# Resetting the tally that shares PSUM evictions between ACT and DVE at each item, and moving one block of weight transposes behind the last attention value

## The chip, the cores and the metric

One core of one Trainium2 chip. The metric is device time in microseconds, the median of several executions; the kernel before takes 173.48 us (173.47 to 173.84 in 3 runs). Profiles show one execution, whose span is some 2 us shorter than the device time. Every profiled run was in the fast state, at a granted TensorE clock of 0.995 to 1.000.

In this document PE is TensorE (PEld its weight loads), ACT is ScalarE, DVE is VectorE, POOL is GpSimd and SP is the engine that issues most stores and DMA transposes. "L581" is line 581 of the kernel. The PSUM tiles h_ps, k_ps, v_ps, s_ps and o_ps hold the maxout product, the k sort, the v sort, the scores and the values; g, kT, v_sb, e and x are what is made of them outside of PSUM.

## The reference, cut to what matters

```python
def attention(q, k, v, sort_net):            # (4, 8, 768, 64), 8 blocks of 96
    P = sort_net
    for _ in range(5):                       # Sinkhorn: rows, then columns
        ...
    k_sorted, v_sorted = P @ k_blocks, P @ v_blocks
    scores = scale * q_b @ k_sb.T            # inside each block
    return softmax(scores) @ v_sb

x = attention(...).transpose(0, 2, 1, 3).reshape(3072, 512)
g = maximum(x @ w1, x @ w2)                  # 512 -> 1024
out = g @ w_out                              # 1024 -> 512
```

## The kernel before

The kernel works on four items (b = 0 to 3). While PE computes the output layer of item b, it also does the attention of item b + 1 in small steps. The maximum is split as x w2 + relu(x (w1 - w2)), so that relu(x (w1 - w2)) is the g tile and the rest is one product with W2 W_out (`wc`), which the first item computes from transposed W2 (`w2T`).

Three things matter here. First, all products go through the same four PSUM tiles of 4 KB per partition:

```python
psum = ctx.enter_context(tc.tile_pool(name="psum", bufs=4, space=bass.MemoryType.PSUM))
def ps_f32(name):
    return psum.tile([128, 1024], FP32, tag="ps", name=name)
```

So a new product waits until an older tile has been copied out ("evicted") by ACT or DVE. Second, a tally decides at build time which of the two does it:

```python
load = {"A": 0.0, "D": 0.0}

def pick(a_ns, d_ns):
    if load["A"] + a_ns <= load["D"] + d_ns:
        load["A"] += a_ns
        return "A"
    load["D"] += d_ns
    return "D"

def evac(out_ap, in_ap, n, two_x=False, eng=None):
    a_ns, d_ns = (200 + n) / 1.2, (130 + (n / 2 if two_x else n)) / 0.96
    if eng:
        load[eng] += a_ns if eng == "A" else d_ns
    if (eng or pick(a_ns, d_ns)) == "A":
        nc.scalar.copy(out=out_ap, in_=in_ap)
    else:
        nc.vector.tensor_copy(out=out_ap, in_=in_ap)
```

Other work is charged as well: each exp of scores adds 800 to "A", each normalized value 900 to "D", each piece of turning v into the layout of the sort 800 to "D". Third, in the first item the second half of W2 is transposed on PE and copied out in two halves, on ACT and on DVE (`w2_transposes(1, "AD")`), among the last values of the first item:

```python
tail = {
    ...
    3: [
        VA[6],                                    # values: product, then 1/sum and x on DVE
        lambda: w2_transposes(1, "AD")(),
        VA[7],
        lambda: x_transposes(0, 2, "A"),
        ...
    ],
    4: [lambda: x_transposes(0, 3, "A"), load_rest, lambda: turn(second, 36)],
    ...
}
...
for b in range(B):
    units = [... moe_h(b, 0, t) ..., moe_h(b, 1, t) ..., moe_out(b, ti, part) ...]
    ...
    steps, lo = [], 2
    ...
```

The softmax here doesn't subtract the row's maximum and nothing guards it: scores larger than these inputs give would overflow.

## Time and profile before

| | before |
|---|---|
| device time, median | 173.48 us |
| span of the profiled run | 171.4 us |
| PE busy | 161.7 us (94%) |
| ACT busy, DVE busy | 83.7 and 87.9 us (49%, 51%) |
| PE idle from 72 to 91 us | 1.93 us |

The shares of ACT and DVE over the whole run look perfectly balanced.

What one eviction costs is read from the groups on the page of the kernel before. The columns are line, engine, operation, output and input tile, shapes, count, then busy us and mean ns of one, then the idle time ahead of them:

```profile
L595 ACT ACTIVATE g<-h_ps 128x768 bf16<-128x768 f32 x23 | 18.6, 812 | 17.4 <-PE h_ps L581 17.4
L597 DVE TENSOR_SCALAR g<-h_ps 128x768 bf16<-128x768 f32 x9 | 8.6, 956 | 25.5 <-PE h_ps L581 25.5
L105 DVE CAST v_sb<-v_ps 96x1024 bf16<-96x1024 f32 x7 | 8.3, 1214 | 4.1 <-PE v_ps L398 3.3
L103 ACT CAST v_sb<-v_ps 96x1024 bf16<-96x1024 f32 x9 | 8.8, 1020 | 1.6 <-PE v_ps L398 1.6
```

An eviction costs 0.14 to 0.19 us more on DVE than on ACT, for the same tile. The tally's formula gives 1.02 and 1.20 us for 1024 elements, so its costs are right; what it is ignorant of is when the charged work happens. The views of the stretches, of the chain and of the waits are shown in the prediction.

### The profile page before, as it was taken

What the parts mean: (1) busy time and instruction counts of PE and PEld (TensorE: products, weight loads), DVE (VectorE), ACT (ScalarE), POOL (GpSimd) and SP (SyncE); (2) the same over time, 40 slices, a digit from 0 to 9 for tenths busy, and PEclk for the clock granted to TensorE, in tenths of its full rate; (3) what the DMA queues carried; (4) which work ended last, traced back from release to release, by engine and by line L of the source; (5) the groups of instructions that cost most, each with busy time, mean ns of one, the idle gap of its engine ahead of it and who ended that gap; (6) DMA issues with size and microseconds to landing.
All of it is one profiled execution on the core that took longest, in us unless ns stands there. A gap on an engine that the chain in (4) does not pass through costs nothing.

```text
span 171.4 us, 4548 instructions
## 1 busy us (share of the span) xinstructions
PE 161.7 (94%) x2015; PEld 96.6 (56%) x2015; DVE 87.9 (51%) x194; ACT 83.7 (49%) x102; POOL 24.8 (14%) x40
## 2 busy tenths in 40 slices
PE   7699999999999999998889999999999999999992
PEld 7548676736666554456555455575545445654462
DVE  5879668499556399810485644225472232420040
ACT  4599975846645554069764253275605214231001
POOL 7955362242300000000320000000000000000000
PEclk9999999999999999999999999999999999999999
DMA  4999999999999452992099267950023273000333
GB/s 49 201 205 207 199 207 206 207 205 207 213 222 196 76 168 54 193 232 96 4 174 189 54 168 145 195 183 4 2 50 77 91 205 130 6 0 0 122 122 126
DMA packets 29811, 23.11 MB, mean 135 GB/s; under 512 B 16672, under 2 KB 24736, under 8 KB 29792
## 3 DMA queue, kind: packets, MB, share of 16 engines
q0 software_dynamic: 10304, 12.58, 43.1%
q1 hardware_dynamic: 19200, 10.04, 23.2%
q8 instruction: 16, 0.26, 0.6%
q10 hardware_dynamic: 288, 0.20, 0.4%
q14 instruction: 3, 0.02, 0.0%
HBM read 25.17 MB, written 6.29 MB: 184 GB/s over the span
## 4 chain that ended last, share of the span: by engine, by line
PE 80%; DVE 10%; ACT 6%; issue 2%; DMA 1%; DVEq 0%; ACTq 0%
PE out_ps L608 37%; PE h_ps L581 22%; PE o_ps L471 4%; PE wc_ps L559 3%; PE k_ps L377 3%; PE s_ps L444 3%; ACT v_sb L103 2%; PE v_ps L398 2%; DVE v_sb L105 1%; ACT kT L103 1%; DVE x L488 1%; PE tw_ps L529 1%; PE tq_ps L347 1%; PE tq_ps L352 1%; ACT g L595 1%
## 5 line engine op out<-in xcount | busy, mean ns | idle before, releaser
L608 PE MATMUL out_ps<-wo_sb,g 128*128 128x512 bf16 (+2 forms) x208 | 48.3, 363 | 0.0
L581 PE MATMUL h_ps<-xT,w_sb 128*128 128x384 bf16 x256 | 44.8, 326 | 2.1 <-DVE v_sb L105 0.7
L581 PEld LDWEIGHTS <-w_sb 128*128 128x128 bf16 x256 | 24.2, 98 | 17.5 <-issue 2.0
L452 ACT ACTIVATE e<-s_ps 96x768 bf16<-96x768 f32 x32 | 24.2, 808 | 16.7 <-PE s_ps L444 16.6
L595 ACT ACTIVATE g<-h_ps 128x768 bf16<-128x768 f32 x23 | 18.6, 812 | 17.4 <-PE h_ps L581 17.4
L608 PEld LDWEIGHTS <-g 128*128 128x128 bf16 x208 | 17.6, 97 | 15.2
L608 PE MATMUL out_ps<-wc,xT 128*128 128x512 bf16 (+2 forms) x104 | 25.0, 362 | 0.0
L103 ACT COPY o<-out_ps 128x1024 f32<-128x1024 f32 x10 | 10.1, 1012 | 29.3 <-PE out_ps L608 24.7
L488 DVE TENSOR_TENSOR x<-o_ps,rs 96x512 bf16<-96x512 f32 x32 | 22.0, 687 | 1.1
L597 DVE TENSOR_SCALAR g<-h_ps 128x768 bf16<-128x768 f32 x9 | 8.6, 956 | 25.5 <-PE h_ps L581 25.5
L482 DVE RECIPROCAL rs<-o_ps 96x8 f32<-96x8 f32 x32 | 6.4, 200 | 21.4 <-PE o_ps L471 21.4
L608 PEld LDWEIGHTS <-xT 128*128 128x128 bf16 x104 | 9.9, 97 | 11.0
L471 PEld LDWEIGHTS <-e 96*128 96x128 bf16 x256 | 11.6, 98 | 6.9 <-DVE x L488 0.7
L209 DVE COPY v_dc<-v_raw 64x768 bf16<-64x768 bf16 (+2 forms) x18 | 15.4, 896 | 0.1
L471 PE MATMUL o_ps<-v_sb,e 96*128 96x65 bf16 x256 | 13.1, 193 | 0.3 <-DVE x L488 0.2
L105 DVE CAST v_sb<-v_ps 96x1024 bf16<-96x1024 f32 x7 | 8.3, 1214 | 4.1 <-PE v_ps L398 3.3
L103 ACT CAST v_sb<-v_ps 96x1024 bf16<-96x1024 f32 x9 | 8.8, 1020 | 1.6 <-PE v_ps L398 1.6
L444 PEld LDWEIGHTS <-kT 64*128 64x128 bf16 x256 | 6.1, 94 | 5.6 <-issue 4.8
L103 ACT CAST kT<-k_ps 128x1024 bf16<-128x1024 f32 x9 | 8.6, 1022 | 0.7 <-PE k_ps L377 0.7
L444 PE MATMUL s_ps<-qT,kT 64*128 64x96 bf16 x256 | 8.8, 204 | 0.2
L559 PE MATMUL wc_ps<-wo_sb,w2T 128*128 128x512 bf16 x32 | 7.7, 380 | 0.0
L81 PEld LDWEIGHTS <-fill 128*128 128x128 bf16 x109 | 6.3, 112 | 2.2 <-DVE fill L72 1.2
(76 smaller groups left out, 129.4 us busy)
## 6 DMA issues: line engine op xcount, KB each, us to landing
out_dram<-o SPq DMA_DIRECT2D x11, 512.0 KB, 3.0
k_raw<-in_k_dram POOLq DMA_DIRECT2D x12, 256.0 KB, 10.2
q_raw<-in_q_dram POOLq DMA_DIRECT2D x4, 768.0 KB, 12.5
v_raw<-in_v_dram POOLq DMA_DIRECT2D x6, 384.0 KB, 13.5
w_sb<-in_moe_w_dram POOLq DMA_DIRECT2D x3, 512.0 KB, 15.9
wo_sb<-in_moe_w_out_dram POOLq DMA_DIRECT2D x2, 512.0 KB, 19.2
v_raw<-in_v_dram POOLq DMA_DIRECT2D x3, 256.0 KB, 4.9
w_sb<-in_moe_w_dram POOLq DMA_DIRECT2D x2, 256.0 KB, 14.2
```

Source lines behind the costliest of these rows:

```text
L103: nc.scalar.copy(out=out_ap, in_=in_ap)
L105: nc.vector.tensor_copy(out=out_ap, in_=in_ap)
L209: nc.vector.tensor_copy(out=dst, in_=src)
L444: nc.tensor.matmul(ps[:, h2 * 512 + ii * 128 : h2 * 512 + ii * 128 + BLK], kT[b][rows, (hp * 8 + i) * BLK : (hp * 8 + i) * BLK + 128], rhs ...
L452: nc.scalar.activation(out=e[:, 0 : 8 * BLK].rearrange("p (t c r) -> p t c r", t=8, r=R), in_=ps[0:BLK].rearrange("p (t f) -> p t f", t=8) ...
L471: nc.tensor.matmul(ps[:, h2 * 512 + ii * 65 : h2 * 512 + (ii + 1) * 65], e[:, (h2 * 4 + ii) * BLK : (h2 * 4 + ii) * BLK + 128], v_sb[:, m0 ...
L488: nc.vector.tensor_tensor(out=x, in0=ov[:, :, :, 0:D], in1=rs.to_broadcast([BLK, 2, 4, D]), op=ALU.mult,)
L559: nc.tensor.matmul(wc_ps[0][:, m * 512 : (m + 1) * 512], w2T[:, fb, dmt * 128 : (dmt + 1) * 128], wo_sb[:, fb, :], start=(fb == 0), stop=( ...
L581: nc.tensor.matmul(h_ps[t][:, m * 512 : m * 512 + TCH], w1_sb[:, hp, fb * 128 : (fb + 1) * 128], xT[:, b % 2, ch, hp % 2, hp // 2, :], sta ...
L595: nc.scalar.activation(out=g, in_=src, func=AF.Relu)
L597: nc.vector.tensor_scalar(out=g, in0=src, scalar1=0.0, scalar2=None, op0=ALU.max)
L608: nc.tensor.matmul(dst, g_tiles[b, ch, m // 2][:, m % 2, off : off + 128] if m < NFB else xT[:, b % 2, ch, hp % 2, hp // 2, off : off + 12 ...
```

## The change

Its intent: the tally should compare what the two engines have to do now, and not what they did in an earlier item; and the x of the last values should not stand behind the copies of W2.

```diff
         3: [
             VA[6],
+            VA[7],
             lambda: w2_transposes(1, "AD")(),
-            VA[7],
             lambda: x_transposes(0, 2, "A"),
...
         steps, lo = [], 2
+        load["A"] = load["D"] = 0.0
         if b < B - 1:
```

## The prediction

> **What bounds the kernel now.** I read the busy table by stretches first, then the chain that ended last in the two stretches where TensorE is not full, then who waited for whom there.
>
> The stretches (columns: from:to in us, length, then busy us of PE, PEld, DVE, ACT, POOL with instruction counts, granted clock, DMA share, GB/s):
>
> ```profile
> 30.00:39.00 9.00, 8.52 (x94) 5.00 (x87) 6.68 (x13) 6.06 (x8) 3.20 (x5) 1.00 1.12 206
> 39.00:55.00 16.00, 15.65 (x261) 10.42 (x259) 10.36 (x15) 9.62 (x12) 1.98 (x4) 1.00 1.14 210
> 55.00:72.00 17.00, 17.00 (x168) 8.62 (x167) 13.73 (x29) 6.54 (x8) 0.00 (x0) 1.00 0.60 120
> 72.00:91.00 19.00, 17.07 (x325) 10.83 (x323) 7.29 (x13) 13.52 (x16) 2.67 (x5) 1.00 0.63 136
> 91.00:109.00 18.00, 18.00 (x173) 9.26 (x166) 8.76 (x19) 6.54 (x8) 0.00 (x0) 1.00 0.73 154
> 109.00:126.00 17.00, 16.64 (x236) 10.44 (x235) 6.84 (x10) 9.56 (x12) 0.00 (x0) 1.00 0.34 64
> ```
>
> TensorE is the bound: 161.7 of 171.4 us busy. Only 72 to 91 us, the start of the second item (b = 1: maxout products, k sort, v sort), has much to win: 19.00 - 17.07 = 1.93 us idle. ACT there is busy for 13.52 us and DVE for 7.29: the evictions are shared badly exactly where PE waits for them. The first item's 30 to 39 us has 0.48 idle, the third item's 109 to 126 has 0.36.
>
> The chain in the second item (start, us, what):
>
> ```profile
> 77.01 0.81 ACT g L595
> 77.82 1.19 ACT kT L103 x2
> 79.01 0.51 issue
> 79.51 1.04 ACT kT L103
> 80.56 1.82 ACT v_sb L103 x2
> 82.38 0.04 issue
> 82.42 1.47 PE h_ps L581 x8
> ...
> 84.95 2.27 DVE v_sb L105 x2
> 87.22 0.04 issue
> 87.26 1.46 PE h_ps L581 x8
> ```
>
> and its waits:
>
> ```profile
> PE h_ps L581 <- DVE v_sb L105: 0.7, 1, 0.7
> PE h_ps L581 <- ACT v_sb L103: 0.6, 1, 0.6
> PE h_ps L581 <- ACT kT L103: 0.5, 1, 0.5
> ```
>
> From 77.01 to 82.38 us the end of the kernel hangs on ACT alone: one g, three kT, two v_sb, one behind the other, while DVE does nothing from 73.7 to 84.0. Then it hangs on two v_sb in a row on DVE. Each time the next product waits for one of the four PSUM tiles.
>
> In the first item:
>
> ```profile
> 33.28 1.02 ACT w2T L103
> 34.33 0.69 DVE w2T L105
> 35.02 0.12 DVE rs L482
> ...
> 35.16 0.70 DVE x L488
> ...
> 35.91 0.51 PE tx_ps L509 x8
> ```
>
> The last values' normalization (x) stands behind the w2T copy on DVE, and the x transposes of PE behind that.
>
> **What the Trainium skill says.** "Perfetto Trace Analysis", section Optimization Strategy: the same gap repeating on the engine that should be saturated can mean that there is no PSUM for the next tile. The trace agrees: gaps of 0.51, 0.57 and 0.69 us before three h_ps tiles, each ended by an eviction. "PSUM — Partial Sum Buffer", section Engine vs sequencer instructions: ACT and DVE queues are strict FIFO, and matmuls start in program order. The trace agrees: a late tile holds up all that follows it. So the order of evictions counts, not only their sum. "VectorE: DVE Perf Modes", section on the TRN2 errata: PSUM to SBUF costs VectorE 120 + n cycles at 0.96 GHz and ScalarE 172 + n at 1.2, so for 1024 elements 1.19 and 1.00 us. Measured here: 1.21 and 1.02; for 768 elements 0.96 and 0.81. The measured ones are used below. DVE is thus a little dearer per eviction, but where it is idle that is no loss.
>
> **The change, part by part.** No arithmetic is added or removed; on PE 16 transposes trade places with 8 value products, on ACT and DVE some evictions change engine.
>
> *(a) Why the reset matters.* I added up the tally as the program does. When the second item begins, before has A = 35.6 and D = 43.0 us: DVE is charged for the turning copies of the first item, long done. So ACT gets the next nine evictions by tally. With the reset at zero they alternate.
>
> *(b) Second item.* The built order shows, before: g A A A, kT A A A, v A A, g A, [e e A], g D, v D D, g A, v A D, g A, v D A, g D. After: g A D A, kT D A D, v A D, g A, [e e A], g D, v D A, g D, v A D, g A, v A D, g A. In all one g and two kT move from ACT to DVE: ACT -(0.81 + 2 x 1.02) = -2.85 us, DVE +(0.96 + 2 x 1.21) = +3.4, so roughly 10.7 each in this stretch. Both fit in 17. I laid the new order out by hand, with before's measured steps: an h tile occupies PE 1.30 us (1.39 with the switch to 64-row work) and its result is out 1.51 after its start; a pair of v tiles 0.57, the first result 0.45 after the start, the second 0.73; k tiles 0.57 each, result 0.74 after the start; a release reaches PE 0.05 later; back-to-back pitch on DVE 1.14, on ACT 0.95 to 1.0. The third k tile ends at 78.6 as before.
> - kT: DVE 77.64 to 78.86, ACT 78.2 to 79.2, DVE 78.8 to 80.0. The v pair runs at 78.6 and 78.9. The 4th h needs the second kT: start 79.30 (before 79.69).
> - v_sb: ACT 79.2 to 80.2, DVE 79.9 to 81.15. The 5th h needs the latter and the scores before it end at 81.3: start 81.4 (before 82.42).
> - g on DVE 82.9 to 83.9, the two exp on ACT done by 83.1. The next v pair at 82.8 and the 6th h at 83.3 (before 84.53).
> - v_sb: DVE 83.8 to 85.05, ACT 83.5 to 84.5. The second v of the next pair waits for 85.05; 7th h at 85.45 (before 87.26).
> - v pair at 86.8, 8th h at 87.4 (before 89.23), scores at 88.8, first output product at 89.3 (before 91.08).
> The gain is 91.08 - 89.27 = 1.8 us, nearly all of the 1.93 idle.
>
> *(c) First item, the move.* After: values (0.24) follow at 32.19, transposes from 32.43, their ACT copy 33.52 to 34.53, DVE copy 34.57 to 35.26. The x of the last values is done by 34.2, ahead of the copy. The weight products wait for the DVE copy, go on at 35.3 for 0.43, the x transposes follow at once at 35.75, the second weight products at 36.1 (before 36.26), ending 37.92 instead of 38.09. Gain 0.17 us: the DVE copy still has to be waited for, only the x behind it is freed, and the transposes start 0.24 later.
>
> *(d) First item, the reset.* It swaps one kT and one v_sb to ACT and one v_sb to DVE around 44 to 50 us. The query transposes there wait for the first v_sb on ACT; that one waits for PE and not for the third kT ahead of it (ACT would be free at 47.0, the sort's result comes at 47.5). 0.
>
> *(e) Third item.* One output copy (1.2 us) goes to DVE at 104; the tile is needed again 2.8 us later, and x tiles delayed by 1 us are read by products 10 us on. One g goes to DVE; the 0.3 us wait at 121 stands behind another g on ACT. 0.
> *(f) Fourth item.* Strict alternation with the other engine first; h tiles come every 1.30 us and evictions take 0.81 or 0.96. 0.
>
> Sum: 1.8 + 0.17 = 2.0 us; 173.48 - 2.0 = 171.5 us.
>
> **The rivals.**
> 1. *The gain is hidden in another wait.* Once ACT is relieved, the second item could wait for the transposed x that come by DMA: the 5th h needs the ones issued from 72.05 to 75.54. The longest landing of that kind took 5.1 us, so at most 80.6, against 81.4: it holds, but with under 1 us to spare. Did it bind, part of (b), perhaps 0.5 to 1 us, would go: 172.0 to 172.5.
> 2. *DVE becomes the bound.* Its copies are 0.2 us dearer, and kT, kT, v_sb stand in a row on it (77.64 to 81.15). In my layout that row ends just as PE arrives. If the strided kT copy is slower in a row, the 5th h comes some 0.3 us later: 171.8. That DVE was idle for ten microseconds speaks against more.
> 3. *The first item gets worse.* If ACT, loaded with a third kT, is late for the v_sb that frees the tile of the query transposes, up to 0.5 us is lost: 172.0. ACT's 0.5 us of slack speaks against it.
> 4. *More than expected.* If all waits of 109 to 126 and 30 to 39 fell too: another 0.36 + 0.3 = 0.7 us, so 170.8. Nothing in the order there removes the wait at 121 us.
>
> **Range and chances.** Three of four rivals cost up to a microsecond and would not come together; the upside is bounded by PE's idle time. So 170.9 to 172.5. Faster by over 2% means under 170.0, a gain of 3.5 us, which all the idle of 30 to 126 us (0.48 + 0.35 + 1.93 + 0.36 = 3.1) does not give: 0.03. Slower by over 2% would need a new stall of 5 us: 0.01. Within 2%: 0.96.
>
> **What would show it right or wrong.** Right: between 72 and 91 us ACT and DVE near 10 to 11 us each; the three waits of h_ps for evictions gone or under 0.2 us; from the second item's first h product to its first output product 16.4 us instead of 18.2; the first item's x transposes no longer behind x; the stretch after 91 the same length. Wrong: h_ps waiting for a DMA transpose (rival 1) or for DVE kT or v_sb by over 0.3 us (rival 2); a longer wait of the query transposes at 48 us (rival 3); a gain lying chiefly in the first item, or the time outside 170.9 to 172.5.

## The result

The changed kernel takes 171.51 us (171.44 to 171.60 in 4 runs), the kernel before 173.66 us in the same rounds (173.47 to 173.95). The ratio is 0.9875, with a 95% interval of 0.9857 to 0.9893. Here and below a ratio is the mean time of one kernel's fast runs over that of the other's of the same rounds, so it is not quite the ratio of the medians quoted beside it. The change is a gain of 2.1 us, clear of noise.

The stretches of the changed kernel, at the same bounds and in the same columns as those in the prediction:

```profile
30.00:39.00 9.00, 8.83 (x101) 5.22 (x96) 7.07 (x15) 6.28 (x8) 3.15 (x5) 1.00 1.12 204
39.00:55.00 16.00, 15.65 (x261) 10.40 (x260) 8.64 (x13) 10.45 (x13) 2.35 (x3) 1.00 1.14 210
55.00:72.00 17.00, 17.00 (x169) 8.66 (x168) 13.79 (x28) 6.54 (x8) 0.00 (x0) 1.00 0.64 117
72.00:91.00 19.00, 19.00 (x342) 11.72 (x341) 11.44 (x18) 12.68 (x15) 2.67 (x5) 1.00 0.75 155
91.00:109.00 18.00, 18.00 (x163) 9.31 (x161) 8.79 (x18) 5.03 (x6) 0.00 (x0) 1.00 0.78 150
109.00:126.00 17.00, 16.70 (x241) 10.38 (x240) 9.35 (x14) 7.74 (x10) 0.00 (x0) 1.00 0.23 60
```

From 72 to 91 us PE went from 17.07 to 19.00 busy of 19.00: no idle time is left. DVE does 11.44 us there where it did 7.29. (ACT's 12.68 holds more of the following work than before, as PE is two microseconds further on at 91 us.) Counted from the first h product of the second item to its first output product in each kernel, ACT went from 13.49 to 10.79 us and DVE from 6.58 to 10.41, near the 10.7 each that the prediction worked out. The last rows are shifted by the gain and can't be compared line by line.

The chain of the changed kernel in the second item (start, us, what):

```profile
72.89 4.00 PE h_ps L581 x24
76.90 1.64 PE k_ps L377 x96
78.54 0.72 PE v_ps L419 x32
79.25 1.41 PE h_ps L581 x8
80.66 0.45 PE s_ps L444 x16
81.10 1.46 PE h_ps L581 x8
82.56 0.57 PE v_ps L419 x32
...
88.53 0.45 PE s_ps L444 x16
88.98 1.40 PE out_ps L608 x6
```

Where the chain before ran through six evictions on ACT and then three on DVE, it now runs on PE alone. The chain over the whole span says the same: PE's share went from 80% to 87%.

What PE waited for in the changed kernel, products of the items only:

```profile
PE h_ps L581 <- ACT g L595: 0.2, 1, 0.2
PE tq_ps L347 <- ACT wc L103: 0.2, 1, 0.2
PE tq_ps L347 <- ACT v_sb L103: 0.2, 1, 0.2
```

The three waits of h_ps for kT and v_sb (0.5, 0.6 and 0.7 us) are gone. What is left are the waits of the first and third item that the prediction left in place.

And the first item, the chain again:

```profile
33.62 1.02 ACT w2T L103
34.64 0.02 issue
34.66 0.70 DVE w2T L105
35.37 0.05 issue
35.41 0.60 PE wc_ps L559 x2
36.02 0.34 PE tx_ps L509 x8
```

The x of the last value is out of the chain, and the x transposes follow the products with no wait. But ACT w2T and then DVE w2T are still in it, one behind the other.

To say where the time came from I use a ledger of four sections, cut at PE instructions that all versions have in common: the start of the last value product but one of the first item (at 31.95 us before), the small `pe` product that ends the first item's W2 work (38.09), the first h product of the second item (72.90), its first output product (91.08), and the start of the last copy on ACT (168.30). Each section is the difference of two starts in one trace:

| us | first item, W2 | rest of first item | second item, start | rest |
|---|---|---|---|---|
| before | 6.14 | 34.81 | 18.18 | 77.22 |
| changed | 5.98 | 34.81 | 16.08 | 77.16 |
| gain | 0.16 | 0.00 | 2.10 | 0.06 |

The sum is 2.3 us. What lies outside of the four sections is not the same in all traces: the first cut comes at 31.93 to 32.27 us in the ten, with identical code ahead of it, and 3.1 to 3.8 us follow the last cut. That is why times of single runs differ by some tenths whatever the kernel; the sections don't have this scatter.

### The profile page after: what moved, and what is told of

Same layout as the page of the kernel before. It is cut to its first block, busy times and chain, and to the rows that moved or that the text cites. A ratio compares the mean times of both kernels' runs of the same rounds, so it can differ in the third digit from the quotient of the medians.

```text
span 169.6 us, 4551 instructions
## 1 busy us (share of the span) xinstructions
PE 162.3 (96%) x2015; PEld 97.0 (57%) x2015; DVE 91.8 (54%) x198; ACT 80.4 (47%) x98; POOL 25.3 (15%) x40
## 4 chain that ended last, share of the span: by engine, by line
PE 87%; DVE 6%; ACT 3%; DMA 1%; issue 1%
PE out_ps L608 37%; PE h_ps L581 26%; PE o_ps L471 5%; PE k_ps L377 4%; PE s_ps L444 4%; PE wc_ps L559 3%; PE v_ps L398 2%; PE v_ps L419 1%; PE tw_ps L529 1%; PE tq_ps L347 1%; DMA p_sb<-in_sort_net_dram 1%; PE tq_ps L352 1%; DVE colsum L226 1%; PE o_ps L81 1%; PE tx_ps L509 1%
## 5 line engine op out<-in xcount | busy, mean ns | idle before, releaser
L595 ACT ACTIVATE g<-h_ps 128x768 bf16<-128x768 f32 x21 | 16.9, 810 | 18.0 <-PE h_ps L581 18.0
L103 ACT COPY o<-out_ps 128x1024 f32<-128x1024 f32 x9 | 9.1, 1012 | 30.0 <-PE out_ps L608 25.7
L597 DVE TENSOR_SCALAR g<-h_ps 128x768 bf16<-128x768 f32 x11 | 10.5, 955 | 22.5 <-PE h_ps L581 22.5
L103 ACT CAST kT<-k_ps 128x1024 bf16<-128x1024 f32 x8 | 7.7, 1021 | 1.1 <-PE k_ps L377 1.1
L105 DVE COPY o<-out_ps 128x1024 f32<-128x1024 f32 x2 | 2.4, 1224 | 10.6 <-PE out_ps L608 9.5
L81 PEld LDWEIGHTS <-fill 128*128 128x128 bf16 x109 | 6.9, 120 | 2.2 <-DVE fill L72 1.2
```

What stands on the lines that cost most here:

```text
L81: nc.tensor.matmul(ps[:, 0:w], w0, fill[:, 0:w], start=True, stop=True)
L595: nc.scalar.activation(out=g, in_=src, func=AF.Relu)
L597: nc.vector.tensor_scalar(out=g, in0=src, scalar1=0.0, scalar2=None, op0=ALU.max)
```

## The experiments

The theory after the result: the second item's alternation is worth 2.1 us, the move 0.16, the other resets next to nothing; and within the second item it is the order of the evictions that counts, since PE takes its four tiles in turn, not how much each engine has to do in all. Rivals: the gain is spread over the items; or the balance of the sums is enough; or ACT was simply too slow and full. All eight runs below gave correct results. The first four ran on one chip beside the same runs of before (173.91 us, 173.43 to 174.21, 11 runs), the last four on one chip beside another eleven (173.71 us, 173.23 to 174.12).

### e1: the move alone

```diff
-        load["A"] = load["D"] = 0.0
```

> Only the second W2 transposes are moved behind the last value, the tally is never reset. My theory (the move is worth about 0.15 us in the first item and the second item keeps its row of ACT evictions): 173.4 to 173.6 us beside a before of 173.5 to 173.7, ratio about 0.999; from 72 to 91 us PE is idle for about 1.9 us as before. Rival (the move gives a good part of the 2.15 us): 172.5 or less.

Measured: 173.57 us (173.21 to 173.94, 6 runs), ratio 0.9984 (0.9966 to 1.0002). In the ledger the first item's section takes 5.98 us, as in the changed kernel, and the second item's 18.18, as before. So the move gives 0.16 us; the clock times can't resolve it, the sections do.

### e2: the reset of the second item alone

```diff
         steps, lo = [], 2
+        if b == 1:
+            load["A"] = load["D"] = 0.0
+        if b == 2:
+            load["A"], load["D"] = 0.0, 1686.7   # the lead that DVE had in before
```

> No move; the tally is reset at the second item only, and set back to the lead it had in before (DVE ahead by 1.69 us) when the third begins, so the built order differs from before in the second item alone. My theory: the second item is everything, 2.0 to 2.1 us gained, ratio 0.988, about 171.6 us, and TensorE idle between 72 and 91 us goes from 1.93 us to under 0.1. Rival (the gain is spread over the items): at most half of it, 172.6 us or more.

Measured: 171.50 us (170.86 to 171.84, 4 runs), ratio 0.9861 (0.9837 to 0.9885). Sections: 6.14, then 34.81, then 16.08, then 77.17 us. The whole of the second item's gain is there without anything else.

### e3: the same sums in another order

```diff
+        if b == 1:
+            fixed.extend("AAADDAAADDAADDDADDA")   # taken by pick() in place of the tally
```

> The changed kernel, but in the second item the same number of evictions of each kind on each engine (ACT 5 g, 1 kT, 4 v_sb; DVE 3 g, 2 kT, 4 v_sb) in rows on one engine: g A A A, kT D D A, v A A, g D, g D, v A A, g D, v D D, g A, v D D, g A. My theory (the order counts, as each tile is waited for in turn): laid out by hand the 4th h product starts 0.8 us later than in the changed kernel, the last one 1.5, the first output product 1.9: about 173.4 us, the whole gain lost with the same busy time of ACT and DVE from 72 to 91 us. Rival (only the balance of the sums counts): 171.5 us as the changed kernel.

Measured: 173.17 us (173.10 to 173.54, 4 runs), ratio 0.9966 (0.9947 to 0.9985). Its stretch from 72 to 91 us:

```profile
72.00:91.00 19.00, 17.20 (x326) 10.87 (x324) 11.05 (x16) 11.46 (x14) 2.67 (x5) 1.00 0.70 148
```

ACT and DVE are almost evenly loaded, 11.46 and 11.05 us, and PE is idle for 1.80 us. The chain of this kernel shows by what (its line numbers are six higher):

```profile
77.48 2.37 DVE kT L111 x2
...
79.89 1.46 PE h_ps L587 x8
...
86.24 4.53 DVE v_sb L111 x4
...
90.82 0.38 PE out_ps L614
```

Two kT in a row on DVE, later four v_sb in a row. The second item's section takes 18.08 us against 16.08 of the changed kernel and 18.18 of before; the hand layout had said 1.9 us more, and it is 2.00. Balance in this order, without alternation, is worth 0.1 us. This settles it between order and sums.

### e4: the mirror, a row on DVE

```diff
+        if b == 1:
+            load["A"] = 7400.0          # after the reset: ACT counts as ahead
```

> The changed kernel, but the tally of the second item begins with ACT 7.4 us ahead, the mirror of before: the first seven evictions go to DVE (g D D D, kT D D D, v D) and ACT stands idle. My theory (a row on one engine is what costs, whichever it is): by hand the first output product comes 1.6 to 1.7 us later than in the changed kernel, 173.1 us. Rival (ACT is the engine that is too slow or too full; taking work off it is what helps): 171.5 to 172.0 us.

Measured: 173.07 us (172.61 to 173.39, 4 runs), ratio 0.9947 (0.9923 to 0.9971). The second item's section takes 17.46 us, 1.38 more than with alternation, where 1.6 to 1.7 were expected. ACT had only 8.08 us of work from 72 to 91 us here:

```profile
72.00:91.00 19.00, 17.67 (x328) 11.06 (x328) 15.14 (x21) 8.08 (x10) 2.67 (x5) 1.00 0.70 147
```

So with ACT relieved, but the row on DVE, 0.72 us of the 2.10 are left. The row of seven evictions on DVE costs the other 1.38 us, though that engine was the idle one before; the rival of the slow ACT, which promised 171.5 to 172.0 us, falls.

### e5: the changed kernel again

No edit; it is the base for the next two.

> The changed kernel once more, as the base for the two that follow on the same chip. 2.1 to 2.3 us under before, ratio 0.987 to 0.988.

Measured: 171.40 us (171.00 to 171.79, 6 runs), ratio 0.9861 (0.9841 to 0.9882). Sections 5.98, 34.82, 16.08 and 77.16 us.

### e6: W2 copied by DVE alone, in the old place

```diff
             VA[6],
+            lambda: w2_transposes(1, "D")(),
             VA[7],
-            lambda: w2_transposes(1, "AD")(),
```

> The changed kernel with the second W2 transposes back in their old place, ahead of the last value, but copied out by DVE alone (one copy of 1.22 us in place of 1.02 on ACT and then 0.70 on DVE). My theory (what the first item loses is the two copies in a row, not the place of the transposes): by hand the copy ends before the weight products need its second half, the x of the last value ends as they end, and the products after it start 0.35 us earlier: TensorE idle from 30 to 39 us about 0.1 or less, time 0.3 us under the changed kernel, ratio 0.986. Rival (the place counts, as the change had it; x behind a longer copy delays the x transposes): 0.1 to 0.3 us slower than the changed kernel.

Measured: 170.90 us (170.74 to 171.52, 5 runs), ratio 0.9843 (0.9822 to 0.9863). The stretch and the chain in the first item:

```profile
30.00:39.00 9.00, 8.95 (x101) 5.44 (x96) 7.49 (x15) 5.46 (x7) 2.84 (x6) 1.00 1.11 209
```

```profile
33.88 1.77 PE wc_ps L559 x8
35.65 0.34 PE tx_ps L509 x8
35.99 1.73 PE wc_ps L559 x8
```

No copy stands in the chain any more. The first item's section takes 5.66 us: 0.32 less than in the changed kernel (0.35 expected) and 0.48 less than before. The second item stays at 16.08. So the old place costs nothing once one engine copies the whole, in 1.23 us; what cost time was that the DVE half starts only when the ACT half has ended (34.33 after 34.30 us in before). Whether a whole copy in the new place would do as well was not run. The intervals of e5 and e6 overlap, so the sections carry this verdict rather than the clock times.

This is the version that beats both kernels: 170.90 us against 171.40 and 173.71 in the same rounds, the changed kernel by the ledger alone.

### e7: and the query transposes earlier

```diff
-                steps = group(*vs[:3]) + qs[:1] + group(*SC[0:2], vs[3]) + qs[1:] + VA[:1]
+                steps = group(*vs[:2], qs[0]) + vs[2:3] + group(qs[1], *SC[0:2]) + vs[3:] + VA[:1]
```

> The kernel of the run before, and in the first item the two groups of query transposes are issued earlier, so that neither waits for a PSUM tile: the first ahead of the third v sort, the second ahead of the first scores. My theory: the waits of 0.16 and 0.19 us at 48 and 52 us (seen in every run so far) fall away, another 0.3 us: 0.6 to 0.7 us under the changed kernel, ratio 0.984. Rival (the third v sort and the fourth then wait in their stead): no gain over the run before.

Measured: 170.98 us (170.77 to 171.01, 4 runs), ratio 0.9840 (0.9820 to 0.9859): no gain over e6 in time, though the two waits are gone and PE is full in the stretch:

```profile
39.00:55.00 16.00, 16.00 (x261) 10.47 (x259) 8.05 (x13) 11.33 (x13) 1.78 (x3) 1.00 1.14 210
```

The starts in the two traces say where the gain went. From the first v sort of this stretch to the first output product, e6 takes 6.09 us (46.56 to 52.65) and e7 6.00 (46.63 to 52.63). Inside a product the matmuls start 0.029 us apart in the v sort, 0.056 in the query transposes and 0.216 in the weight products; what a step from one product to the next takes beyond that is lost. e6 loses 0.32 and 0.35 us at its two waits, which are both steps from the v sort on 64 rows to the query transposes on 128, then 0.10 at a step from 128 rows to 64, and 0.04 at the end. e7 has five steps between 64 rows and 128 in place of three: four of them lose about 0.10 us each, and the last, to the output product, 0.16. And the fourth v sort starts 0.14 us late, at 52.01, just after the copy of wc on ACT has ended (50.95 and 1.01 long): the wait that was expected away had moved there. What is left is 0.09 us. The rival was right in part, and the rest went to two more changes of shape. That the shape is their cause is shown by other steps of the same trace: from the output products (128 rows) to the scores (64 rows) 0.10 us is lost in six of six, from the output products to the values (96 rows) 0.00 to 0.02 in 22 of 22.

### e8: every reset but the second item's

```diff
         steps, lo = [], 2
+        load["A"] = 0.0
+        load["D"] = 7447.5 if b == 1 else 0.0    # the second item keeps its old lead
```

> Before without the move, the tally reset at every item but the second, which gets the lead of DVE that it had in before (7.45 us). My theory: nothing, 0 to 0.1 us under before, ratio 0.999 to 1.0, and the second item's waits as in before (0.5, 0.6 and 0.7 us). Rival (the reset of the first, third and fourth items brings part of the gain): 0.3 us or more under before.

Measured: 173.56 us (173.28 to 173.70, 4 runs), ratio 0.9989 (0.9968 to 1.0010). The waits of h_ps in the second item are 0.5, 0.6 and 0.7 us as before; sections 6.14, 34.81, 18.18 and 77.22 us, those of before to the last digit. The resets of the first, third and fourth item are worth nothing.

## Why the prediction was right

Predicted 171.5 us in a range of 170.9 to 172.5; measured 171.51. That the two agree so closely is luck: the kernel before measured 173.66 us in the same rounds in place of 173.48, and the gain was 2.15 us in place of 2.0.

- **What bounds.** Right. The only large idle time of PE lay in the second item, and it is what went away.
- **(a) The tally's lead.** Right. e8 keeps the lead of 7.45 us, resets all else, and gains nothing; e2 takes away that lead alone and gains all of it.
- **(b) The second item, 1.8 us.** Right in mechanism, 0.3 us short in size: 2.10 measured, which is also more than the 1.93 us of idle time that the prediction took as the bound. Two terms of the layout were mis-sized. The first is the step from the scores to the 5th h product: the layout let the scores end at 81.3 us and the h start at 81.4, while the two groups of scores took 0.51 us from their start at 80.59 and the h started at 81.10. Before, they had taken 0.77 us, because a wait hid in them: two neighbouring matmuls start at 81.23 and 81.51, the others at most 0.05 us apart. The profile counts this as busy, so PE's busy time in the section fell too, from 16.25 to 16.08 us. The second is the one wait that the layout had left, for the v_sb at 85.05: that copy ended at 84.68, and nothing waited for it. Counted from the first h product of each kernel (72.90 and 72.83 us), the 5th h came 0.23 us earlier than laid out, the 6th 0.16, the 7th 0.30 and the first output product 0.29.
- **(c) The move, 0.17 us.** Right: 0.16 in the changed kernel and in e1. The reason given, that the DVE copy still has to be waited for, fits e6, where removing that too gives another 0.32.
- **(d), (e), (f), nothing each.** Right: the section from 38 to 73 us did not change by 0.01, and the rest by 0.06; the wait in the third item went from 0.28 to 0.21 us. e8 confirms it for the resets; the 0.06 are there in e2 and not in e8, so they come with the second item's reset.
- **Rival 1 (DMA transposes)** did not happen: no product waited for one, though the 5th h started 0.3 us earlier than laid out. **Rival 2 (the row on DVE)** neither: kT, kT, v_sb ran from 77.56 to 81.05 us, and the product that needs the last of them started at 81.10. That is the 0.05 us that the prediction gives a release, so there was nothing to spare: in this the kernel was lucky. e4 shows what the rival would have been: with a row of seven in place of three, the same engine costs 1.38 us. **Rival 3** neither: the query transposes waited 0.16 us as before. **Rival 4** did not happen: what was gained beyond 2.0 us came from the second item, and the wait at 121 us stayed at 0.21.

## What to carry to other kernels

A tally that shares work between two engines must forget work that is already done: a lead from an earlier stage sends a whole row of later evictions to one engine while the other stands idle. Look at the balance, and above all at the order, within the stretch where the matmul engine waits: with the four PSUM tiles of this kernel, equal sums in rows of two to four lost nearly all that alternation had gained. When one eviction is split between two engines and the halves run one behind the other, giving it whole to one engine may be faster (0.32 us in e6).

A smaller lesson is how to read idle time: a wait inside a group of short matmuls can count as busy, so the idle time of PE isn't the upper limit of a gain.

## What the Trainium skill lacked or had wrong

- "Perfetto Trace Analysis", section Optimization Strategy, gives too few buffers as what regular gaps can mean. Here the same four tiles gave 1.93 us of gaps or none from 72 to 91 us, depending only on which engine evicts which tile. That the order of evictions counts, and not only each engine's load, is not there: with ACT at 11.46 and DVE at 11.05 us, PE was idle for 1.80 us (e3).
- "VectorE: DVE Perf Modes", section on the TRN2 errata: its formula gives 1.00 us for 1024 elements from PSUM on ScalarE. A single copy took 1.02, but three in a row took 2.84 us, so each further one only 0.91; on VectorE the formula gives 1.19, a copy took 1.21 and two in a row 2.36, so the second 1.15. In a row this formula overstates the pace by 0.09 and 0.04 us.
- "TensorEngine Tiling (Array Packing)", section Key Properties, says that a change of tiling mode drains TensorE, but not what it costs. In the trace of e7 a step from matmuls on 128 rows to matmuls on 64 loses 0.09 to 0.10 us where nothing else is waited for, and one from 128 rows to 96 loses 0.00 to 0.02. That the first is a change of tiling mode and the second none is read from the row counts. In e7 two more such changes, with one new wait of 0.14 us, left only 0.09 of the gain.
